# Ten dummy matmuls in four hops, and another spread of two chunk inversions

## The chip, the core and the metric

The kernel runs on one core of one Trainium2 chip. The metric is the device time of one execution in microseconds (us); lower is better. The engines of the core run side by side and wait for each other by semaphores: TensorE (PE: matmuls, with PEld for its weight loads), VectorE (DVE), ScalarE (ACT), GpSimd (POOL) and SyncE (SP), which issues most of the DMAs.

## The reference

A delta-rule attention (4 batches, 8 heads, 768 positions, head size 48) is followed by a feed-forward block with a quick GELU (384 to 2048 to 384) over the 3072 tokens:

```python
k_n = k / (np.linalg.norm(k, axis=-1, keepdims=True) + 1e-06)
state = np.zeros((B, H, D, D))
for t in range(S):
    y[:, :, t] = einsum('bhd,bhde->bhe', q[:, :, t], state)
    v_old = einsum('bhde,bhd->bhe', state, k_n[:, :, t])
    state = state + beta * einsum('bhd,bhe->bhde', k_n[:, :, t], v - v_old)
x = y.transpose(0, 2, 1, 3).reshape(B * S, H * D)
h = x @ w_in
out = (h * (1.0 / (1.0 + np.exp(-1.702 * h)))) @ w_out
```

The two weights arrive as 64-bit floats, and the kernel converts them itself.

## The kernel before, in words

**Units.** The sequence is cut into 6 chunks of 128 positions. A chunk of one batch, with all 8 heads, is a unit; unit n is chunk n // 4 of batch n % 4, so there are 24. Inside a chunk the recurrence is a triangular system. Its four diagonal 32x32 blocks per head are inverted on DVE (`invert`, L460), and the rest is solved by blocks on PE: `solve` multiplies a block of values V with the inverse XB, `below` multiplies the result with the Gram matrix G into psR, and `rest` (L665) subtracts psR from V on DVE, so that the next block can be solved. `together` (L862) puts one such hop of two or three units side by side. From chunk 1 on, `scores` also gives psQ, of which a part is subtracted from V.

**Inversion.** `invert` is a generator that is advanced by hand, with `ahead_of(inverting, n)` for n groups and `run(inverting)` for what is left. From chunk 2 on it works on two units at a time (64 partitions) in 25 groups: one multiplies NT, the Gram blocks, by beta; 15 small ones are each a TENSOR_TENSOR and a TENSOR_REDUCE that grow from 64x2 to 64x450; four make NT from P and four make YB from P (64x256 to 64x1024); the last one makes YS and issues four DMAs on SP: two of YS to DRAM (Yd) and two back into XB, turned.

**Feed-forward.** It is cut into generators too: `hidden` (ph, then GELU to gT), `written` (po, then the output), and `all_written` (L794) for the first chunk. `all_written` runs while w_out is still being converted on DVE (`conversion`): after every two matmuls of po it calls `fill(3)`, three steps of conversion, and, where not all three could be made, one group of the inversion.

**Order.** Up to chunk 2, nearly all instructions are pinned to the order in which the Python code makes them, and each engine works strictly in its order. After the opening the code makes these parts: two hop paths of 8 hops each for the four units of chunk 0 (L1078 to L1084 for the first pair, where `warm` adds dummy matmuls on a bf16 identity, which nobody reads), then a loop of 22 steps (L1139 on) that inverts chunk 1 and feeds PE with ph, with the norms of unit 9 (`ninth`, three steps), and then `woven(n)` for n = 3 to 24, called a slot here. A slot has three hops. The first carries unit n alone with the last blocks of unit n - 1, the second starts unit n + 1, and after the third the outputs of unit n - 1 are formed. Feed-forward work is put between the hops (`spend`). SOON (L904) and STEPS (L903) say how many groups of the inversion follow the first hop, the second hop, and the outputs.

Units 8 and 9 are inverted from slot 4 on. What is left of it after slot 6 is issued at once there:

```python
        if n % HB == 0 and n > B:
            run(inverting)
```

The inversion of units 10 and 11 starts in slot 7, and its last groups are issued at the end of slot 8. Unit 8's inverse is first needed in the second hop of slot 7, that of unit 10 in the second hop of slot 9.

`prepare` (L420) is run within a slot for unit n + 5: it transposes its keys, makes G (half copied from PSUM by ACT, half by DVE), and writes G through DRAM (Nd) into NT; the second of these DMAs waits on SP for the first to land. In slot 6 it is issued ahead of what `run(inverting)` adds. The keys are normalized before that (`normalize_mixed`, from slot 7 on `normalize`): ssq and rn on DVE, a power on POOL, and a product that gives KN.

Of the kernel before, what the change touches and what calls it, by code (L numbers as in the profile page):

```python
# [18 lines left out]
def kernel(  # L19
# [21 lines left out]
    B, H, S, D = q.shape  # L41
# [16 lines left out]
    NW, NY, NU = 14, 26, 11  # L58
# [81 lines left out]
    def warm(n):  # L140
        ps = ps_moe.tile([128, 256], F32, tag="moe", name="ps_warm")
        for _ in range(n):
            pe.matmul(ps, lhsT=ones[:, 0:128], rhs=ones, start=True, stop=True)
# [52 lines left out]
    def fetch_out(f):  # L196

        if f in outside:
            slot = outside[f]
            if slot not in slots and slot[:2] == "gT":  # L200
                slots[slot] = spare("raw").bitcast(I32)[:, 0 : 2 * DM]
            elif slot not in slots:
                slots[slot] = wk.tile([128, 2 * DM], I32, tag=slot[:2].strip("2"), name="raw", bufs=3)
            words = slots[slot]
        else:
            words = raws[:, inside[f] * DM : (inside[f] + 2) * DM]
        places[f] = as_raw(words, (1, DM))
        if order.index(f) >= FC // 2:
            asked[1][f] = asked[0]
        other_queue(  # L210
            out=as_rows(places[f])[:, 0], in_=moe_w_out[f * 128 : (f + 1) * 128, :]
        )
# [95 lines left out]
    def fill(n):  # L308
        all_done = True
        for _ in range(n):  # L310
            asked[0] += 1
            all_done = next(converting, False) and all_done
        return all_done
# [142 lines left out]
    def spare(name):  # L456
        t = wk.tile([128, FQ, NTH], F32, tag="gT", name=name, bufs=GB)
        return t.rearrange("p f t -> p (f t)")
# [334 lines left out]

    def all_written(c, gTs):  # L794

        turns[1] = turns[2] = True
        po = [
            (ps_moe if i < HB else ps_seq[1]).tile([128, DM], F32, tag="moe" if i < HB else "seq", name="po")
            for i in range(B)
        ]  # L800
        for n, f in enumerate(order):
            ahead = order[min(n + 2, FC - 1)]
            while ("out", ahead - ahead % 2 if 4 <= ahead < 8 else ahead) not in done:
                fill(1)
            for i in range(B):
                pe.matmul(
                    po[i], lhsT=gTs[i // HB][f // FQ][:, f % FQ, i % HB * C : (i % HB + 1) * C],
                    rhs=w_out[:, f, :], start=(n == 0), stop=(n == FC - 1),
                )
                if i % HB == HB - 1 and (n < FC - 1 or i < B - 1):  # L810
                    if not fill(3):
                        ahead_of(inverting, 1)
                    yield 1.3
            if f == 3:
                fetch_out(9)
                fetch_out(13)
        turns[2] = False
        rest = spare("o")
        os = [wk.tile([128, DM], F32, tag="o", name="o") for _ in range(HB)]
        os += [rest[:, i * DM : (i + 1) * DM] for i in range(HB)]  # L820
        for i in (2, 3, 0, 1):
            act.copy(os[i], po[i])
        for i in (2, 3, 0, 1):
            beside(out=out[i * S + c * C : i * S + (c + 1) * C, :], in_=os[i])
        yield 1.3
# [15 lines left out]
    def ahead_of(work, n):  # L841
        for _ in range(n):
            next(work, None)
# [18 lines left out]
    def together(solves, belows):  # L862

        solves = [(X, blk) for X, blk in solves if X]
        belows = [(X, blk) for X, blk in belows if X]
        psU = bank("psU") if solves else None
        psR = bank("psR") if belows else None
        for h in range(H):
            for X, blk in solves:
                X.solve(blk, h, psU)  # L870
            for X, blk in belows:
                X.below(blk, h, psR)
        for X, blk in solves:
            X.solved(blk, psU)
        for X, blk in belows:
            X.rest(blk, psR)
# [24 lines left out]
            debt[0] -= done  # L901

    STEPS = (9, 5, 3, 3, 3, 3)  # L903
    SOON = {B - 1: (0, 0, 0), B: (0, 3, 3), B + 1: (1, 1, 1), B + 2: (1, 2, 2)}  # L904
    begun = {}

    def woven(n, share):
# [18 lines left out]
        ahead = STEPS[:3] if n % HB == 1 else STEPS[3:]  # L926
        ahead = SOON.get(n, ahead)

# [95 lines left out]
    def values_scaled(s, hs):  # L1024
        for h in hs:
            act.mul(s.V[:, h, :], s.V[:, h, :], zs[:, 4, s.b, h : h + 1])
# [48 lines left out]
    for i in range(2 * NB):  # L1075
        together(*next(path))
        ahead_of(preparing, 1)
        fill(1 + i % 2 if i else 5)  # L1078
        if 4 <= i < 8:
            values_scaled(pair[HB + (i - 4) // 2], range(i % 2 * NP, i % 2 * NP + NP))  # L1080
        if i in (3, 5):
            pair[HB + (i - 3) // 2].select()
        warm(NU if i < 3 else NU // 2)
        ahead_of(preparing, 1)  # L1084
    for n, s in enumerate(pair[:2]):
        put_out(s, 2 - n)
# [8 lines left out]
    def feed(n=1):  # L1095
        for _ in range(n):
            while ffn and next(ffn[0], None) is None:
                ffn.pop(0)
# [39 lines left out]
    ninth = normalize_mixed(2 * B + 1)  # L1138
    for i in range(22):  # L1139
        ahead_of(inverting, 1)  # L1140
        if i in (14, 17, 20):
            next(ninth)
        if i < 18:
            feed()
        if i in (2, 3, 4, 7, 8, 9, 10):
            fetch_out(i - 2 if i < 5 else i - 3)
# [3 lines left out]
    def beside_conversion(work):  # L1150
        for cost in work:
            fill(4 if ("in", 3, 1) in done else 2)
            yield cost

    queue = [beside_conversion(w) for w in ffn] + [all_written(0, gTs)]
    for n in range(B - 1, len(units) + 1):
        woven(n, 20.8 if n > 6 else 13.0)
# [32 lines left out]
```

## Time and profile before

| | |
|---|---|
| runs | 769.76, 770.48, 774.15 us, median 770.48 |
| the profiled execution | 768.38 us, of which the span of instructions is 766.7 |
| PE busy | 743.1 us, 97% of the span |
| DVE busy | 438.1 us, 57% |
| mean granted TensorE clock | 0.98 |
| ps_warm in the hops (42 to 85 us) | 84 matmuls |

By stage of the kernel, from the answers for single stretches (us busy):

| stretch, us | PE | DVE | clock | what runs |
|---|---|---|---|---|
| 0 to 42 | 34.71 | 33.66 | 0.67 | opening, chunk 0 inverted |
| 42 to 100 | 51.65 | 51.55 | 1.00 | both hop paths |
| 100 to 140 | 39.96 | 37.11 | 1.00 | chunk 1 inverted, ph |
| 140 to 190 | 48.57 | 45.86 | 1.00 | slots 4 to 6, conversion of w_out |
| 190 to 202 | 8.81 | 10.76 | 0.86 | the rest of slot 6's inversion |
| 202 to 245 | 41.56 | 22.59 | 1.00 | slots 7 and 8 |
| 245 to 767 | 517.83 | 236.53 | 1.00 | the other slots, and feed-forward at the end |

A time beside an engine's instruction says how long it was busy; the bracket at the end of a line of the timeline gives the idle time of that engine before it, and what ended it. The TensorE clock is granted by the chip, 1.00 being full speed.

### The profile page before, as it was taken

The page shows a single profiled execution, that of the slowest core. Times are in us where ns is not written, and L with a number is a line of the kernel's source. Part 1 is how long each engine was busy: PE and PEld are TensorE (multiplying, and loading weights), DVE is VectorE, ACT ScalarE, POOL GpSimd, SP SyncE. Part 2 cuts the span into 40 slices and gives each one's busy share as a digit, 9 for nine tenths or more (in the row PEclk, how much of TensorE's full clock was granted, in tenths as well). Part 3 has the DMA queues.
Part 4 walks back from the last instruction along what each step waited for, and adds up shares of the span by engine and source line. Part 5 has one row for each costly group of instructions (what it writes and reads, how often), then busy time and mean ns, then how long its engine had stood idle before and what let it go on. Part 6 is the DMA issues. An engine that isn't in the chain of part 4 may idle for free.

```text
span 766.7 us, 19461 instructions
## 1 busy us (share of the span) xinstructions
PE 743.1 (97%) x8508; PEld 558.2 (73%) x8508; DVE 438.1 (57%) x896; ACT 239.8 (31%) x535; POOL 134.0 (17%) x141
## 2 busy tenths in 40 slices
PE   7888999999899999999999999999999999999998
PEld 6666788666577687687688678678678677687684
DVE  6999898999556566566566566566566521000000
ACT  4557524433233233233133133124123132121110
POOL 6133301312012122122132121230200000000000
PEclk8599999999999999999999999999999999999999
DMA  9965355632332232132142142042030020000000
GB/s 163 174 117 113 82 152 131 165 89 58 65 85 56 56 75 56 42 90 56 36 95 57 35 96 56 23 109 57 22 81 10 23 43 2 17 11 1 27 1 21
DMA packets 131125, 50.78 MB, mean 66 GB/s; under 512 B 106432, under 2 KB 127040, under 8 KB 131040
## 3 DMA queue, kind: packets, MB, share of 16 engines
q1 hardware_dynamic: 127424, 37.34, 23.5%
q0 software_dynamic: 3040, 11.41, 5.6%
q8 instruction: 67, 1.10, 0.6%
q10 hardware_dynamic: 576, 0.79, 0.3%
q14 instruction: 18, 0.15, 0.1%
HBM read 32.08 MB, written 16.25 MB: 63 GB/s over the span
## 4 chain that ended last, share of the span: by engine, by line
PE 77%; DVE 13%; issue 5%; ACT 2%; POOL 2%; DMA 2%; DVEq 0%; POOLq 0%; ACTq 0%; SPq 0%
PE po L102 30%; PE ph L102 26%; PE psY L102 5%; PE psU L102 4%; PE psQ L102 3%; DVE P L102 3%; PE psR L102 2%; PE psG L102 2%; DVE YB L102 2%; PE psT L102 2%; DVE tmp L102 1%; DVE NT L102 1%; DVE w_out L102 1%; DVE w_in L102 1%; POOL rn L102 1%
## 5 line engine op out<-in xcount | busy, mean ns | idle before, releaser
L102 PE MATMUL po<-w_out,gT 128*128 128x384 f32 x768 | 262.5, 493 | 0.0
L102 PE MATMUL ph<-xT,w_in 128*128 128x256 f32 x1152 | 261.4, 383 | 0.3
L102 PEld LDWEIGHTS ph<-xT,w_in 128*128 128x128 f32 x1152 | 214.7, 190 | 32.5 <-issue 1.7
L102 PEld LDWEIGHTS po<-w_out,gT 128*128 128x128 f32 x768 | 142.2, 191 | 92.3 <-issue 3.7
L102 DVE TENSOR_TENSOR V<-V,psR 128x384 f32<-128x384 f32 (+2 forms) x72 | 40.1, 557 | 190.4 <-PE psR L102 189.6
L102 ACT ACTIVATE gT<-ph 128x512 f32<-128x512 f32 x96 | 56.6, 596 | 146.2 <-PE ph L102 146.0
L102 ACT COPY US<-psU 32x384 f32<-32x384 f32 x92 | 43.2, 470 | 145.9 <-PE psR L102 78.3
L102 DVE TENSOR_TENSOR P<-NT,YB 64x8 f32<-64x8 f32 (+26 forms) x178 | 84.3, 474 | 4.7 <-DVE YB L102 0.3
L102 PEld LDWEIGHTS psU<-V,XB 32*32 32x32 f32 x1536 | 58.4, 104 | 36.3 <-issue 26.5
L102 DVE TENSOR_REDUCE YB<-P 64x4 f32<-64x8 f32 (+27 forms) x178 | 77.2, 434 | 6.1
L102 PE MATMUL psU<-V,XB 32*32 32x48 f32 x1536 | 69.7, 203 | 4.4 <-DVE V L102 4.2
L102 PE MATMUL psR<-US,G 32*32 32x48 f32 x2576 | 62.8, 204 | 1.0 <-issue 0.5
L647 POOL TENSOR_SCALAR_AFFINE_SELECT M<-M 128x1024 f32<-128x1024 f32 x20 | 26.5, 1326 | 195.4 <-DVE M L102 161.0
L102 PEld LDWEIGHTS psR<-US,G 32*32 32x32 f32 x2576 | 53.4, 104 | 2.0 <-issue 1.3
L102 PE MATMUL psQ<-QS,kT 48*128 48x176 f32 (+1 forms) x384 | 38.7, 343 | 3.6 <-ACT QS L102 3.6
L102 PEld LDWEIGHTS psQ<-QS,kT 48*128 48x128 f32 x384 | 31.9, 209 | 7.3 <-ACT QS L102 5.4
L102 DVE TENSOR_TENSOR P<-NT 64x256 f32<-64x256 f32 (+7 forms) x44 | 36.3, 824 | 0.4
L102 DVE TENSOR_REDUCE NT<-P 64x64 f32<-64x1024 f32 (+7 forms) x44 | 35.3, 803 | 1.5
L102 PE MATMUL psG<-kT 48*128 48x128 f32 x384 | 32.1, 304 | 1.2 <-ACT G L102 1.2
L87 POOL DMA_DIRECT2D KN<-in_k_dram x13 | 12.4, 950 | 114.8 <-PE psY L102 105.7
L102 ACT COPY o<-po 128x384 f32<-128x384 f32 x24 | 11.4, 479 | 61.5 <-issue 37.3
L102 ACT COPY M<-psQ 128x256 f32<-128x256 f32 x68 | 23.0, 376 | 23.8 <-DVE V L102 17.7
(102 smaller groups left out, 614.8 us busy)
## 6 DMA issues: line engine op xcount, KB each, us to landing
Nd<-G SPq DMA_DIRECT2D x16, 512.0 KB, 3.5
QP<-in_q_dram SPq DMA_DIRECT2D x24, 192.0 KB, 4.0
V<-in_v_dram SPq DMA_DIRECT2D x24, 192.0 KB, 3.3
out_dram<-o SPq DMA_DIRECT2D x20, 192.0 KB, 2.0
raw<-in_moe_w_out_dram POOLq DMA_DIRECT2D x9, 384.0 KB, 3.9
KN<-in_k_dram POOLq DMA_DIRECT2D x14, 192.0 KB, 3.5
w_out<-in_moe_w_out_dram POOLq DMA_DIRECT2D x7, 384.0 KB, 4.8
NT<-Nd SPq DMA_DIRECT2D x20, 128.0 KB, 2.6
```

The source lines that it names most:

```text
L87: dma(out=dst[n % len(dst)][:, :, 0:D], in_=src[b, :, c * C : (c + 1) * C, :].rearrange("h p d -> p h d"),)
L102: return lambda *a, **kw: tc.keep_in_program_order(op(*a, **kw))
L647: (pool if self.n < B else nc.gpsimd).affine_select(out=self.M, in_=self.M, compare_op=ALU.is_gt, fill=0.0, base=0, pattern=[[0, H], [1, 1 ...
```

## The change

1. In hops 3 to 6 of the first pair, `warm` makes 10 dummy matmuls instead of 5, 20 more in all.
2. In `all_written`, a group of the inversion follows only every second time that `fill(3)` could not make all its steps.
3. In slot 5, two groups follow at each of the three places instead of one.
4. In slot 7, the inversion of units 10 and 11 gets 0, 9 and 5 groups at the three places; before it was 9, 5 and 3 by STEPS.
5. The second and third step of `ninth` are called at i = 15 and 19 instead of 17 and 20.

```diff
     def all_written(c, gTs):
 
+        spare_turns = [0]
         turns[1] = turns[2] = True
...
                 if i % HB == HB - 1 and (n < FC - 1 or i < B - 1):
-                    if not fill(3):
+                    spare_turns[0] += not fill(3)
+                    if spare_turns[0] > 1:
+                        spare_turns[0] = 0
                         ahead_of(inverting, 1)
                     yield 1.3
...
-    SOON = {B - 1: (0, 0, 0), B: (0, 3, 3), B + 1: (1, 1, 1), B + 2: (1, 2, 2)}
+    SOON = {B - 1: (0, 0, 0), B: (0, 3, 3), B + 1: (2, 2, 2), B + 2: (1, 2, 2), B + 3: (0, 9, 5)}
...
-        warm(NU if i < 3 else NU // 2)
+        warm(NU if i < 3 else NU - 1 if i < 7 else NU // 2)
...
-        if i in (14, 17, 20):
+        if i in (14, 15, 19):
             next(ninth)
```

In the order of the built programs, TensorE's instructions are the same but for the 20 dummies. On DVE the same instructions stand in another order from the start of the inversion of units 8 and 9 to the end of that of 10 and 11. On SP, the four DMAs of Yd and XB of units 8 and 9 move from between the DMAs of xT to behind the DMA NT<-Nd of slot 6. On ACT one copy to NT moves, that of the inversion of units 10 and 11, from ahead of slot 8's first hop to behind its copies of M.

## Prediction, made before the changed kernel ran

> **What bounds the kernel now.** I read the page first: shares, then slices.
>
> ```profile
> PE 743.1 (97%) x8508; PEld 558.2 (73%) x8508; DVE 438.1 (57%) x896; ACT 239.8 (31%) x535; POOL 134.0 (17%) x141
> ...
> PE   7888999999899999999999999999999999999998
> ...
> DVE  6999898999556566566566566566566521000000
> ```
>
> PE is full from slice 13 (about 245 us) to the end, DVE nearly full from 20 to 200 us. PE's instructions keep their order and number but for the dummies, so the time changes by what PE's idle and slow-clock time changes. I therefore listed PE's idle times after 42 us in the timeline, with what ended each; these are from slots 6 and 7, with the same po x8 of slot 5 ahead of them.
>
> ```profile
> 177.28 2.85 PE L102 MATMUL po<-w_out,gT 128*128 128x384 f32 x8
> ...
> 193.93 0.95 PE L102 MATMUL psT<-ident,KN 128*128 128x128 f32 x4 [2.07 <-DVE KN L102]
> 194.68 4.18 PE L102 MATMUL po<-w_out,gT 128*128 128x384 f32 x8
> ...
> 201.29 0.66 PE L102 MATMUL psY<-QS,ST 48*64 48x128 f32 x14 [0.63 <-DVE V L102]
> ...
> 224.27 0.66 PE L102 MATMUL psT<-ident,KN 128*128 128x128 f32 x4 [1.33 <-POOL KN L331]
> ```
>
> PE stood 2.07 us for the keys of KN. Then eight po took 4.18 us, in slot 5 2.85. The windows say why:
>
> ```profile
> 190.00:194.00 4.00, 1.93 (x41) 0.99 (x30) 3.69 (x10) 0.94 (x2) 0.00 (x0) 1.00 0.26 49
> 194.00:198.00 4.00, 4.00 (x10) 2.55 (x11) 3.93 (x5) 0.60 (x1) 0.00 (x0) 0.57 0.00 0
> ```
>
> The third column from the right is the granted clock: after the pause it fell to 0.57. What DVE did meanwhile is in its timeline.
>
> ```profile
> 190.44 0.41 DVE L102 TENSOR_TENSOR P<-NT,YB 64x256 f32<-64x256 f32 x1
> 190.88 0.41 DVE L102 TENSOR_REDUCE NT<-P 64x64 f32<-64x256 f32 x1
> 191.39 0.42 DVE L102 TENSOR_TENSOR P<-NT 64x256 f32<-64x256 f32 x1
> 191.84 0.41 DVE L102 TENSOR_REDUCE YB<-P 64x64 f32<-64x256 f32 x1
> 192.28 0.56 DVE L102 TENSOR_TENSOR V<-V,psR 64x384 f32<-64x384 f32 x1
> ...
> 193.32 0.56 DVE L102 TENSOR_TENSOR KN<-KN,rn 128x384 f32<-128x384 f32 x1
> ...
> 203.88 0.36 DVE L102 TENSOR_TENSOR ST<-psY,ST 128x192 f32<-128x192 f32 x1 [2.64 <-ACT xT L102]
> ...
> 209.90 0.56 DVE L102 TENSOR_TENSOR V<-V,psR 32x384 f32<-32x384 f32 x1 [4.61 <-PE psR L102]
> ...
> 217.07 1.22 DVE L102 TENSOR_TENSOR NT<-NT,bI 64x1024 f32<-64x1024 f32 x1 [4.94 <-DMA NT<-Nd]
> ```
>
> V and KN queue behind groups of the inversion that nobody needs yet, while DVE stands idle for 2.64 and 4.61 us soon after. And in slot 7 the inversion of units 10 and 11 stands at DVE's head and waits 4.94 us for its DMA, with V and rn behind it; POOL's KN waits for rn, PE for KN (1.33).
>
> **What the Trainium skill says.** "TensorE: Matmul & The Clock Gate", "What's actually happening": the clock has a half-rate and a full state, judged over free-running windows of about 3.4 us of PE activity. The trace agrees in kind: 0.57 in the window above. As its phase is free, other executions may drop elsewhere; no run shown says where. "DMA: Bandwidth & Descriptors", "Two DMAs through the same engine are not ordered": a dependent DMA has to wait for the first one's semaphore; so here SP issues NT<-Nd at 213.87, 4.9 after Nd<-G (208.96). "Perfetto Trace Analysis", "Identifying the Most-Contended Engine", warns that busy PE is not PE at its peak; hence I count only idle and slow time, not shares.
>
> **The change part by part.**
>
> *Dummies.* Eleven ps_warm in a row take 1.38 us and five 0.72, so one costs 0.11 and five more 0.55 a hop. They stand ahead of waits for V of 1.18, 0.62, 0.53 and 1.03 us in hops 3 to 6: hidden but for some 0.02. Without that cover it would be 20 x 0.11 = 2.2 us. The clock is 1.00 throughout 42 to 100 us in this execution, so nothing is gained in its sum. In others a drop there may be avoided; I bound that from 0 to 1.7 us, the price of the drop above.
>
> *Steps of `ninth`.* No engine's order changes by it: the inversion has ended by i = 14. Zero.
>
> *Slots 4 and 5.* I laid the new DVE order over the old times, each instruction not before its producer. NT<-NT,bI (1.21) moves from 147.09 to behind KN (153.5), and DVE loses that time, since it waits for a DMA of w_out at 151.57 anyway. The small groups that go out balance it, but a w_out step that ACT answers comes 0.4 later, and ACT's QS behind it; psQ at 160.10 slips by 0.4, its second half for V by 0.1 more. Loss: 0.5. The later V of slots 4 and 5 come at 158.2, 170.0 and 174.3, each when PE needs it or before.
>
> *Slot 6.* Seven groups and YS were done or queued ahead of the last V. Now V 64x384 comes right after psR (190.9 with the loss above), rn and KN end at 192.5, and PE wants KN at 192.4. The 2.07 gap shrinks to 0.15, and its drop of the clock goes: psT 0.95 - 0.66 = 0.3 and po 4.18 - 2.85 = 1.3. The wait for V ahead of psY (0.63) goes too. Gain: 1.9 + 1.6 + 0.6 = 4.1. The groups of 64x256 and 64x512 (2.2) fit into the idle 2.64 ahead of ST. 64x768, 64x1024 and YS (1.9 + 2.4 + 1.2 = 5.5) follow G, in a hole of 4.6: V 32x384 of slot 7 comes 0.9 late. Behind it waits the second half of psQ; usually V ends about 0.2 ahead of it, so PE loses 0.7.
>
> *SP.* Yd and XB of unit 8 now go behind NT<-Nd. Counted from the end of psG (204.52 before): xT's six issues, then Nd<-G at +3.1; it lands in 3.5 to 4.8, NT is issued at +7.4, Yd at +7.8, lands in 2 to 4, XB is issued at +10.4 to 12 and lands in 2.7 to 4: +13.2 to 16. Slot 8 has the same sequence and comes to about +13. Unit 8's solve follows psG by 219.27 - 204.52 = 14.75, with the 0.7 above 15.4. I take no wait; the bounds are -0.6 late to +2.2 early. What waits behind it would be PE itself.
>
> *Slot 7.* rn stands ahead of NT<-NT,bI now, KN comes 2.0 us before psT: the 1.33 gap goes. NT's DMA, its G earlier, lands before DVE gets there. Eight groups end some 1 us before the next V is due.
>
> *Slot 8.* Now five groups, 0.8 + 1.4 + 1.9 + 2.4 + 1.2 = 7.8, follow G where before there were two (3.7); the hole to V of slot 9 is about 7.1, so by the same reckoning psQ loses 0.45. Later slots are unchanged.
>
> Sum: gains 4.1 + 1.3, losses 0.5 + 0.7 + 0.45: 3.8 us off 768.38, which is 764.6. The median of the runs lies 2.1 above that execution; for the changed kernel I allow half of it, since the dummies and the missing pause leave the clock less to drop at: 765.6.
>
> **The rivals.**
>
> *XB late (no change).* The DMAs behind NT take the long end, unit 8 waits 2 us, the clock drops once (1.7): 765.6 + 3.7 = 769.3. For it: only 1.5 us of margin, and output DMAs land at the same time. Against: slot 8 does the same in time.
>
> *Dummies in the way (no change).* The V of the hops come earlier than in this execution, the dummies show for 2.2: 767.8. Against: all four gaps end with DVE V, and DVE hardly idles there.
>
> *Slower.* SP holds Yd until NT can be issued; if Nd<-G waits for G or its traffic, XB slips one for one. It decides once it lands 1.5 us after the reckoned time; the gain is eaten after about 2 more with a drop of the clock, and at 7.5 late, 765.6 + 7.5 + 1.7 = 774.8, the kernel is slower than can be mistaken. For it: the queue is blocking; against: the longest landing of any of these DMAs here is 4.9.
>
> **How the numbers follow.** The forecast has 0.60, XB late 0.17, the dummies 0.12, slower 0.11. About 0.5% (3.9 us) can be told from no change, so faster means below 766.6. The forecast's own range is 763 to 767.5, nine tenths of it below the bound; with a few hundredths from the rivals, faster 0.56, same 0.33, slower 0.11. The range runs from 762.8 (a drop in the hops avoided, no psQ waits) to 769.8, which takes in both milder rivals.
>
> **What would show it.** Right: no PE idle over 0.3 us before psT of slot 6, clock 1.00 from 186 to 204 us, no wait for KN in slot 7, PE's wait before psQ of slots 7 and 9 under 1 us, hops of the first pair as long as before. Wrong: PE waiting for XB in slot 7, a new drop of the clock, a longer first pair, or PE idling between 140 and 180 us by more than 1 us over before.

## The result, and the profile after

| | before | after |
|---|---|---|
| runs | 769.76 to 774.15 us, median 771.09 (4) | 762.70 to 763.34 us, median 763.11 (4) |
| ratio | | 0.989, 95% interval 0.986 to 0.9921 |
| the profiled execution | 768.38 us | 763.34 us |
| PE busy, DVE busy | 743.1, 438.1 us | 744.1, 438.6 us |

The kernel became 1.1% faster. Forecast were 765.6 us, 0.9937 of the median then known. The two profiled executions differ by 5.0 us, the medians by 8.0. These are two quantities, and they are taken one by one below.

The timeline of TensorE after the change, slots 6 and 7 (start, duration, instruction, idle time before and what ended it):

```profile
191.58 0.66 PE L102 MATMUL psT<-ident,KN 128*128 128x128 f32 x4 [0.28 <-DVE KN L102]
192.07 2.75 PE L102 MATMUL po<-w_out,gT 128*128 128x384 f32 x8
...
206.48 0.86 PE L102 MATMUL psQ<-QS,kT 48*128 48x176 f32 x6 [0.48 <-DVE V L102]
...
219.23 0.66 PE L102 MATMUL psT<-ident,KN 128*128 128x128 f32 x4 [0.33 <-POOL KN L331]
```

The pause of 2.07 us is 0.28, the eight po take 2.75 instead of 4.18, the wait of 1.33 for KN in slot 7 is 0.33, and one wait is new: 0.48 ahead of the second half of psQ. The windows of the same stretch show no drop of the clock. (A line of a window gives its length, then the busy us of PE, PEld, DVE, ACT and POOL, each with its instructions, then the clock, the DMA share and GB/s.)

```profile
190.00:194.00 4.00, 3.72 (x14) 2.06 (x14) 3.83 (x8) 1.41 (x3) 0.00 (x0) 1.00 0.25 49
194.00:198.00 4.00, 3.51 (x121) 2.65 (x119) 3.59 (x8) 0.47 (x1) 0.00 (x0) 1.00 0.02 4
```

DVE's timeline after the change:

```profile
189.93 0.56 DVE L102 TENSOR_TENSOR V<-V,psR 64x384 f32<-64x384 f32 x1 [0.46 <-PE psR L102]
...
204.61 1.22 DVE L102 TENSOR_TENSOR YS<-YB,bI 64x1024 f32<-64x1024 f32 x1
205.86 0.56 DVE L102 TENSOR_TENSOR V<-V,psR 32x384 f32<-32x384 f32 x1
...
216.24 0.56 DVE L102 TENSOR_TENSOR V<-V,psR 64x384 f32<-64x384 f32 x1 [8.14 <-PE psR L102]
```

V of slot 6 now waits for PE (0.46) and not PE for it. The rest of the inversion fills the hole up to YS, and V of slot 7 follows YS without a break: that is where the new 0.48 comes from. In slot 7 DVE waits 8.14 us for PE, where it waited 4.94 for NT's DMA before.

SyncE's queue shows the transfers that were moved behind NT<-Nd:

```profile
207.41 0.33 SPq L102 DMA_DIRECT2D NT<-Nd  x1
207.82 1.31 SPq L102 DMA_DIRECT2D Yd<-YS  x2
211.62 1.00 SPq L102 DMA_DIRECT2D XB<-Yd  x2
```

The first XB lands 2.6 us after its issue, at 214.2; its solve starts at 215.24 without a wait. The margin is 1.0 us.

To place the 5.0 us I compared the start of every DVE subtraction of V in both profiles; "V stands at -0.56" means that it starts 0.56 us earlier than in the profile of before. The changed kernel stands at +0.2 us in the first hop path, at -0.65 us at 135 us, -0.56 in the first hop of slot 6, -4.92 in its third, -5.4 in the first hop of slot 8, -5.11 from its third on and to the end. (In between a single V may lie off by up to 1 us.) The lines behind the largest step, the third hop of slot 6, are these, first before and then after the change:

```profile
199.43 1.22 DVE L102 TENSOR_TENSOR YS<-YB,bI 64x1024 f32<-64x1024 f32 x1
200.68 0.56 DVE L102 TENSOR_TENSOR V<-V,psR 128x384 f32<-128x384 f32 x1
```

```profile
195.76 0.56 DVE L102 TENSOR_TENSOR V<-V,psR 128x384 f32<-128x384 f32 x1 [0.31 <-PE psR L102]
```

Before, V followed the last group of the inversion without a break; now DVE waits for PE.

### The profile page after: what moved, and what is told of

Its sections match the earlier page's. It is cut to its first block, busy times and chain, and to the rows that moved or that the text cites. A ratio compares the mean times of both kernels' runs of the same rounds, so it can differ in the third digit from the quotient of the medians.

```text
span 761.6 us, 19501 instructions
## 1 busy us (share of the span) xinstructions
PE 744.1 (98%) x8528; PEld 559.7 (73%) x8528; DVE 438.6 (58%) x896; ACT 239.9 (31%) x535; POOL 134.4 (18%) x141
## 4 chain that ended last, share of the span: by engine, by line
PE 82%; DVE 8%; issue 5%; ACT 2%; POOL 2%; DMA 1%; POOLq 0%; DVEq 0%; ACTq 0%
PE po L102 29%; PE ph L102 27%; PE psY L102 5%; PE psU L102 5%; PE psQ L102 5%; PE psG L102 3%; PE psT L102 3%; PE psR L102 3%; PE ps_warm L102 2%; DVE w_out L102 2%; DVE tmp L102 1%; DVE V L102 1%; DVE w_in L102 1%; DVE YB L102 1%; DVE P L102 1%
## 5 line engine op out<-in xcount | busy, mean ns | idle before, releaser
L647 POOL TENSOR_SCALAR_AFFINE_SELECT M<-M 128x1024 f32<-128x1024 f32 x20 | 24.4, 1220 | 192.8 <-DVE M L102 160.2
L102 PEld LDWEIGHTS psG<-kT 48*128 48x128 f32 x384 | 28.0, 210 | 3.6 <-ACT G L102 2.1
```

What stands on the lines that cost most here:

```text
L102: return lambda *a, **kw: tc.keep_in_program_order(op(*a, **kw))
L647: (pool if self.n < B else nc.gpsimd).affine_select(out=self.M, in_=self.M, compare_op=ALU.is_gt, fill=0.0, base=0, pattern=[[0, H], [1, 1 ...
```

## The experiments

All were measured against the kernel before in the same series. Each series (e1 to e4, e5 to e8, e9 to e12) ran on a chip of its own; the medians of before differ by up to 1.1 us between them. "Low clock" counts executions whose mean granted clock is 0.971 or less.

| label | what | median us (runs) | span of the runs | low clock | ratio, 95% interval |
|---|---|---|---|---|---|
| e1 | dummies alone | 770.08 (22) | 767.2 to 772.5 | 0 | 0.998, 0.9965 to 0.9996 |
| e2 | all but the dummies | 765.51 (10) | 764.6 to 770.5 | 1 | 0.9932, 0.9907 to 0.9958 |
| e3 | slot 7 alone | 769.23 (22) | 767.2 to 773.0 | 3 | 0.9978, 0.9961 to 0.9996 |
| e4 | slots 4 to 6 alone | 765.24 (8) | 764.2 to 772.0 | 3 | 0.9933, 0.9901 to 0.9965 |
| e5 | the changed kernel | 764.69 (6) | 763.5 to 766.2 | 0 | 0.9926, 0.9909 to 0.9942 |
| e6 | changed, no dummies in hops 3 to 7 | 764.50 (6) | 763.9 to 765.5 | 3 | 0.9923, 0.9908 to 0.9937 |
| e7 | all_written alone | 766.95 (9) | 765.9 to 769.0 | 4 | 0.9959, 0.9945 to 0.9972 |
| e8 | changed, 17 dummies in slots 5, 6 | 763.16 (5) | 762.9 to 763.8 | 0 | 0.9906, 0.9891 to 0.992 |
| e9 | before, the pause filled | 771.42 (14) | 769.4 to 774.3 | 4 | 0.9997, 0.9978 to 1.0016 |
| e10 | the changed kernel | 763.39 (6) | 762.9 to 765.1 | 0 | 0.9894, 0.9866 to 0.9921 |
| e11 | as e8 | 763.40 (6) | 762.7 to 763.9 | 0 | 0.9888, 0.9861 to 0.9915 |
| e12 | as e8, 1, 2, 3 groups in slot 6 | 762.46 (6) | 762.2 to 763.0 | 0 | 0.9879, 0.9852 to 0.9906 |

The kernel before had medians of 770.72 (49 runs), 770.23 (14) and 771.35 (19) in the series of e1 to e4, e5 to e8 and e9 to e12. Of these 82 runs 34 have a low clock, with a median of 773.8; the 8 with 0.979 or more have 768.3. So its profiled execution (768.38, clock 0.98) was one of its best.

**e1: the dummies alone**

```diff
-        warm(NU if i < 3 else NU // 2)
+        warm(NU if i < 3 else NU - 1 if i < 7 else NU // 2)
```

> The kernel before with the 20 dummies alone. Two theories of the 3 us that the runs gained over what the two profiled executions show (768.38 to 763.34, so 5.0, while the medians went from 771.1 to 763.1, so 8.0). Theory A: the dummies hold TensorE's clock in executions in which it falls in the first pair; then this gains about 3.0 (ratio 0.996) and the clock of every execution is 1.00 between 42 and 100 us. Theory B: the pause in slot 6 costs some executions more than the profiled one; then the dummies alone give nothing (ratio 1.000), and the runs scatter over several us as those of before.

Median 0.6 us less, and none of 22 runs has a low clock where 20 of the 49 beside them have: theory A in kind, but with a gain of 0.3 to 2.7 by the interval, less than its 3.0. The scatter of several us stays, as theory B has it. The profiled execution is one of the longest (771.95): its clock falls at 174 to 178 us and at 201 to 208, and V loses 2.7 and 2.6 us there (more under e9). The hops themselves are no shorter: every V from 47 to 76 us stands at about +0.17. A step of 0.75 comes at 77 to 80 us, in the second pair, far from any edit. The timeline of before shows what is missing there afterwards:

```profile
78.18 0.20 PE L102 MATMUL psR<-US,G 32*32 32x48 f32 x1
78.21 0.20 PE L102 MATMUL psU<-V,XB 32*32 32x48 f32 x1
78.96 0.23 PE L102 MATMUL psR<-US,G 32*32 32x48 f32 x2 [0.54 <-issue]
```

In the middle of a hop TensorE stops for 0.54 us with nothing that the profile shows to wait for. From the second V of the second pair to the third it is 2.75 to 3.32 us in the six profiles with the old dummies, of which before's is the longest, 2.46 to 2.59 in the seven with the new, and 2.57 without any in hops 3 to 7 (e6). But most of the step comes without the new dummies too: e3, e7 and e9, with the old ones, show 0.54 to 0.58 us of it against before, and the view lists no such stop in them. It lists one in before, e2 (0.48) and e4 (0.25). So the dummies can be given the 0.2 to 0.3 us that every profile with the old ones is longer; that they also keep the stop away (none in seven, against three in six) is likely and not shown. What TensorE stops for was not settled.

**e2: all but the dummies**

The whole change without e1's line.

> All of the change but the dummies. Theory A: 5.0 us less than before by the profile's gain, ratio 0.9935, with a scatter of several us left. Theory B: all 8.0 us, ratio 0.9896, and runs within 1 us of each other.

5.2 us less by the medians: theory A's number, and the scatter is there. The profiled execution happened to be the longest of the ten (770.47). Its windows show why:

```profile
174.00:178.00 4.00, 2.40 (x29) 1.77 (x26) 3.90 (x10) 0.59 (x2) 0.00 (x0) 0.71 0.02 4
178.00:182.00 4.00, 4.00 (x45) 3.68 (x41) 2.07 (x6) 1.33 (x5) 0.91 (x1) 0.50 0.04 6
182.00:186.00 4.00, 4.00 (x7) 2.18 (x8) 3.09 (x6) 0.59 (x1) 0.00 (x0) 0.51 0.61 174
```

The clock falls in slot 5 and stays at half for some 10 us. The V ahead of it stands at +1.97 against before's profile and the first of slot 6 at +6.61: 4.6 us for one drop. TensorE's timeline has two waits close together there, 0.61 for ACT and 0.99 for V before psY. So the clock can fall in slot 5 too, and in some executions only: the profiles of e1, e3, e5 and e7 have a shorter drop between 162 and 178 us, the other nine have none in slot 5.

**e3: slot 7 alone**

```diff
-    SOON = {..., B + 2: (1, 2, 2)}
+    SOON = {..., B + 2: (1, 2, 2), B + 3: (0, 9, 5)}
```

> The kernel before with the entry for slot 7 alone (0, 9, 5 groups). Both theories: PE's wait of 1.33 us for the keys KN in slot 7 goes or falls to 0.3, the pause of 2.07 in slot 6 with its slow clock stays: 1.0 to 1.3 us less (ratio 0.9985), which is near what can be told apart.

The wait for KN is 0.33, and V moves from +2.16 in slot 6 to +1.08 in slot 8: 1.1 us, as reckoned. The medians give 1.5, within the interval.

**e4: slots 4 to 6 alone**

```diff
-                    if not fill(3):
+                    spare_turns[0] += not fill(3)
+                    if spare_turns[0] > 1:
+                        spare_turns[0] = 0
...
-    SOON = {B - 1: (0, 0, 0), B: (0, 3, 3), B + 1: (1, 1, 1), B + 2: (1, 2, 2)}
+    SOON = {B - 1: (0, 0, 0), B: (0, 3, 3), B + 1: (2, 2, 2), B + 2: (1, 2, 2)}
```

> The kernel before with the edits to slots 4 to 6 alone (every second group in all_written, 2, 2, 2 in slot 5). Pause and slow clock in slot 6 go. By the prediction's sum the wait for KN in slot 7 stays, and this gains 2.7 in the profile; theory A then 2.7 to 3.7 in the medians, theory B 6.7. A third reading: NT of units 10 and 11 lands some 6 us earlier here, so that it holds up nothing in slot 7 even ahead of V and rn; then this alone gives what the spread gives, and the entry for slot 7 adds nothing to it.

The median is e2's within 0.3, so the third reading holds for the time as far as these runs can tell. It holds only half for its reason. NT still made DVE wait 4.49 us:

```profile
213.29 1.22 DVE L102 TENSOR_TENSOR NT<-NT,bI 64x1024 f32<-64x1024 f32 x1 [4.49 <-DMA NT<-Nd]
...
218.40 0.56 DVE L102 TENSOR_TENSOR V<-V,psR 64x384 f32<-64x384 f32 x1
```

V and KN follow late behind it, yet PE's wait for KN is 0.34 as in e2. In the profile the entry for slot 7 is worth 0.6 us on top of this part (V from slot 6 to the end: 0.4 lost here, 0.2 gained in the changed kernel), of 1.1 alone.

**e5 and e10: the changed kernel again**

> The changed kernel once more, on one chip with the others of this row. If the four runs that it has (762.7 to 763.3) are what it always gives, the median stays at 763.1 and the scatter under 1 us. If they happened to meet no drop of the clock, the median is 764 to 765 and some runs lie at 766 to 770, as with the parts; then the ratio is nearer 0.992 than 0.989.

> The changed kernel a third time, beside the next two on one chip: by its ten runs so far 763.6, with some runs at 766 in which the clock fell in slots 5 or 6.

764.69 and 763.39. With its first four runs it has 16, median 763.5; ten of them lie below 764, the longest is 766.22. The four of the result were on the good side, but the second ratio is again 0.989: there the kernel before is 1.1 us longer than beside e5, with 10 of 19 low clocks in place of 4 of 14, and the changed kernel is 1.3 shorter. The profile of e5 has a drop in slot 5, at 174 to 178 us, and V goes from -0.41 to +1.13 there; that of e10 has none.

**e6: no dummies at all in hops 3 to 7**

```diff
-        warm(NU if i < 3 else NU - 1 if i < 7 else NU // 2)
+        if i < 3:
+            warm(NU)
```

> The changed kernel with no dummy matmuls at all in hops 3 to 7 of the first pair (45 fewer). If the dummies hold TensorE's clock there: drops to 0.5 within 50 to 70 us in the profile, more runs with a mean clock of 0.97 or less, 2 to 5 us more than the changed kernel. If the hops are only waits for DVE and the clock doesn't depend on them: the same time as the changed kernel within 0.5 us, with the hops as long as before.

Both readings are half right. The clock falls, from 54 to 70 us, the longest drop of any profile here:

```profile
54.00:62.00 8.00, 6.56 (x94) 5.70 (x95) 7.64 (x14) 6.82 (x18) 4.55 (x4) 0.58 0.82 183
62.00:70.00 8.00, 8.00 (x93) 7.24 (x91) 7.12 (x13) 6.02 (x17) 2.28 (x1) 0.56 0.38 67
```

And it costs little. V stands at -0.36 against before at 47 us, and at the same -0.36 at 61: up to there DVE, busy for 7.64 of the 8 us, sets the pace, and a TensorE at half speed keeps up. Behind that TensorE is busy all the time, and the next V, the first of the second pair, waits for it (in the changed kernel it doesn't) and stands at +0.53:

```profile
74.31 0.55 DVE L102 TENSOR_TENSOR V<-V,psR 128x384 f32<-128x384 f32 x1 [0.97 <-PE psR L102]
```

Part of this comes back. From 47 to 85 us e6 loses 0.55 to 0.66 us to the profiles with the new dummies (the changed kernel, e1, e5, e8, e10 to e12), which have no stop at 79 us either. Against the profile of before, which has the stop, nothing shows: -0.52 at 85 us. The median, 764.50, is that of e5 beside it; 0.6 us is less than these runs can tell.

So a low mean clock alone is hardly a loss. In kernels with the old dummies it goes with longer times all the same (e7: 767.8 to 769.0 for its four, 765.9 to 767.0 for the others). The profile of e7 has a drop at 62 to 67 us that costs nothing (V at +0.48 ahead of it, at +0.25 behind) and one at 162 to 165, around which V goes from +0.60 to +1.88. No execution with a low clock and the old dummies was profiled, so where those runs lose their time stays open.

**e7: all_written alone**

The first four lines of e4's diff (and the line that sets spare_turns to 0).

> The kernel before with the edit of all_written alone (a group of the inversion every second time). V and KN of slot 6 no longer stand behind the inversion, so the pause of 2.07 us and its slow clock go. But some 8.5 us of groups now follow G, where the hole in DVE is 4.6: V of slot 7 comes about 3.9 late and psQ waits 3.5 for it. By my reckoning of holes this gains 4.1 and loses 3.5: 770 against 770.7. If instead the wait of psQ is hidden, it gains like the edits to slots 4 to 6 together: 765.2.

766.95, and neither number. The reckoning of DVE's hole is right: V of slot 7 moves from -1.83 to +2.04, 3.9 late. But PE waits only 0.98 ahead of psQ, and for something else:

```profile
210.07 0.86 PE L102 MATMUL psQ<-QS,kT 48*128 48x176 f32 x6 [0.98 <-ACT US L102]
```

So a late V doesn't hold psQ one for one, though the expectation had it so. Slot 6 gains 3.7 (V from +1.88 to -1.83). The first V of slot 7 is late, the ones behind it are not: from slot 7's second V to the end they stand at -1.49, so that slot 7 as a whole costs 0.3.

**e8 and e11: 17 dummies in slots 5 and 6**

`warm` takes the PSUM tile as a second argument here and in e9.

```diff
         turns[1] = turns[2]
+        if n == B + 1:
+            warm(9, ps_big.tile([128, 256], F32, tag="big", name="ps_warm"))
         run(D_.scored)
...
         if A:
+            if n in (B + 1, B + 2):
+                warm(4, ps_big.tile([128, 256], F32, tag="big", name="ps_warm"))
             A.queries()
```

> The changed kernel with 17 dummies more in slots 5 and 6: 9 ahead of psQ of slot 5, where PE waits 1.05 us, and 4 each ahead of psY, where it waits 0.5 to 0.8. If the scatter of the runs comes from the clock falling after these thin stretches (as the profiles of two parts show at 162 to 178 us), the runs lie closer together and no profile has a clock of 0.5 between 150 and 190 us; the dummies themselves cost 0 to 0.5. If the clock falls by chance or for another reason, the scatter stays that of the changed kernel.

> The changed kernel with the 17 dummies in slots 5 and 6, again. If these dummies keep the clock up: all runs within 1 us at 763.2, none above 764.5, while the changed kernel beside it has runs above 764.5. If its five runs were luck: the same scatter as beside it.

Eleven runs in two series lie between 762.73 and 763.89, none with a drop in slots 5 or 6 in its profile; of the changed kernel's 16 runs six lie above. The median hardly moves (763.4 against 763.5 over all runs; 763.16 against 764.69 and 763.40 against 763.39 beside each other). In these runs the dummies take away the long ones and cost nothing that can be measured.

**e9: the pause filled**

```diff
         spend(share / 6)
+        if n == B + 2:
+            warm(17, ps_big.tile([128, 256], F32, tag="big", name="ps_warm"))
         next(P, None)
```

> The kernel before with 17 dummies ahead of psT of slot 6, so that TensorE is busy in the pause of 2.07 us while DVE's order, and so the pause itself, stay. If the slow clock behind the pause is made by the pause, the clock stays 1.00 from 190 to 204 us, the eight po after it take 2.85 us and not 4.18, and the kernel gains the 1.6 us of the prediction: 768.6 to 769 where before has 770.2 to 770.7, with V of the later hop now the next thing to wait for, since DVE's burst ends when it did: then part of the 1.6 comes back as a wait for V ahead of psY (0.6 before, up to 2.2 now), and the gain is between 0 and 1.6. If the clock falls in any case, nothing is gained.

The kernel before, with TensorE busy in the pause; its timeline:

```profile
191.34 2.02 PE L102 MATMUL ps_warm<-ident 128*128 128x256 bf16 x17
193.57 0.66 PE L102 MATMUL psT<-ident,KN 128*128 128x128 f32 x4 [0.21 <-DVE KN L102]
194.06 2.75 PE L102 MATMUL po<-w_out,gT 128*128 128x384 f32 x8
...
200.94 1.12 PE L102 MATMUL psY<-QS,ST 48*64 48x128 f32 x14 [2.33 <-DVE V L102]
```

The clock stays up and the eight po take 2.75. Nothing is gained: PE reaches psY earlier, waits 2.33 us for V instead of 0.63, and the clock falls there instead, from about 200 to 206 us.

That the pause makes the slow clock isn't shown by this. In the profile of e1 the pause is open, 2.07 us as in before, and yet the clock stays up behind it and falls only at the longer wait for V:

```profile
195.28 0.66 PE L102 MATMUL psT<-ident,KN 128*128 128x128 f32 x4 [2.07 <-DVE KN L102]
195.77 2.75 PE L102 MATMUL po<-w_out,gT 128*128 128x384 f32 x8
...
202.65 1.13 PE L102 MATMUL psY<-QS,ST 48*64 48x128 f32 x14 [2.32 <-DVE V L102]
```

```profile
196.00:200.00 4.00, 3.51 (x89) 2.07 (x88) 3.93 (x5) 1.04 (x2) 0.00 (x0) 1.00 0.01 4
200.00:204.00 4.00, 1.68 (x20) 1.10 (x22) 2.53 (x3) 0.00 (x0) 0.00 (x0) 0.69 0.29 65
204.00:208.00 4.00, 4.00 (x46) 3.91 (x44) 0.36 (x1) 0.81 (x3) 0.94 (x1) 0.50 0.01 1
```

In e3 the clock falls after the open pause as in before (eight po in 4.34 us). So behind an open pause it fell in two of three profiles.

V itself doesn't depend on all this: it stands at -0.35 all through slot 6 in e9 and at +1.36 all through slot 6 in e1. TensorE's waits for KN and V, 2.07 and 2.32 in e1, are together the same 4.4 us as 2.07, the 1.6 of the slow clock and 0.63 in before. The 4.4 us that the changed kernel gains in slot 6 are DVE's lateness, and PE's slow clock was inside them. Where the clock falls at the wait for V, it costs more on top: against before, V of slot 7 stands 2.5 (e9) and 2.6 us (e1) later than V of slot 6 did. So slot 6 can cost an execution more than the profiled one, as theory B of e1 has it.

**e12: one group more ahead of ST**

```diff
-    SOON = {..., B + 2: (1, 2, 2), B + 3: (0, 9, 5)}
+    SOON = {..., B + 2: (1, 2, 3), B + 3: (0, 9, 5)}
```

> The same, with three groups instead of two at the last place of slot 6, so that 64x768 stands ahead of ST and G and only 64x1024 and YS follow G. DVE has 0.56 us of idle time ahead of ST; V of slot 7 comes that much earlier, and PE's wait of 0.48 ahead of psQ in slot 7 goes. If that wait is on the path: 0.5 less than with 17 dummies alone, 762.7. If G, 1.3 us later, holds up Nd and with it XB: no gain or some tenths lost.

This is e11 with one group more at the last place of slot 6. It takes 0.94 us less than e11 beside it, where 0.5 was expected; the runs of the two overlap only from 762.7 to 763.0. It takes 0.9 less than the changed kernel. DVE's and TensorE's timelines:

```profile
203.52 1.22 DVE L102 TENSOR_TENSOR YS<-YB,bI 64x1024 f32<-64x1024 f32 x1
204.98 0.56 DVE L102 TENSOR_TENSOR V<-V,psR 32x384 f32<-32x384 f32 x1 [0.24 <-PE psR L102]
```

```profile
204.84 1.62 PE L102 MATMUL psQ<-QS,kT 48*128 48x176 f32 x16
```

V of slot 7 waits for PE again, and psQ runs through in 1.62 us. In the changed kernel its two parts took 1.16 and 0.86 with 0.48 between them, from 204.84 to 207.34: the late V cost 0.88 us, and not only the wait. V stands at -4.92 here and at -4.04 there. This kernel is faster than both before and the changed one.

## Why the prediction was right or wrong

**Slot 6: right in place and size.** Foreseen were 4.1 us, V moved by 4.36 (-0.56 to -4.92). The parts were named by TensorE's waits: 1.9 pause, 1.6 clock, 0.6 V. e9 and e1 show that they can't be had one by one; it is one quantity, how late DVE is with V. Where all of DVE's lateness goes, the sum over PE's waits gives the same number. That the sum came out right doesn't show that each part was a gain of its own.

**Slot 7: right in its parts.** KN's wait fell by 1.0 (1.3 foreseen); V of slot 7 is 0.88 late (0.9) and costs psQ 0.88 (0.7), of which 0.48 is a wait. XB came in time with 1.0 us to spare (1.5): the rival "XB late" didn't come. On SP, Nd<-G was issued 4.3 us after the end of psG, not 3.1, and XB at 12.0, the late end of its range.

**Slots 4, 5, 8 and 9: too pessimistic for this execution.** For slots 4 and 5 0.5 us of loss were laid down; V moves from -0.65 to -0.56, 0.1. That is in part luck: with the same slots 4 and 5 it loses 0.1 to 0.65 in e4, e6, e8, e10, e11 and e12, which have no drop there, and 1.8 in e2 ahead of its drop. For slot 9 0.45 were laid down; V there is 0.55 late, and 0.55 earlier again at the next, so PE lost nothing. Within slot 8, where no loss was foreseen, 0.3 are lost.

**The dummies: hidden, as said, in all four hops.** Of the profile's 5.0, 0.65 arises at 77 to 80 us, for which the prediction has no term. A good part of it is luck: before's profiled execution was the longest there of the six with the old dummies, and three of the others were 0.54 to 0.58 shorter. The dummies' own part is 0.2 to 0.3, as far as the profiles show it.

So the sum came to 5.0 in place of 3.8: 0.65 from outside the argument, 0.4 from the loss in slots 4 and 5 that was charged and not taken, 0.3 from slot 6. Slots 7 to 9 together gave 0.2, as charged; their errors cancel.

**The step that failed is the allowance for the clock:** "The median of the runs lies 2.1 above that execution; for the changed kernel I allow half of it". The median of the four runs lay 0.2 below the changed kernel's own profiled execution, so the distance was not halved but gone; over 16 runs the median is 0.2 above. Of the 2.5 us between the forecast and the measured median, 1.3 are in this term and 1.2 in the sum above. The mechanism was named, a clock with less to drop at, and its size was taken too small. It was half the distance of one execution from a median of three, and that execution was among the best tenth of 82, while the runs of before reach up to 778. With 5.0 in the sum and no distance left the forecast would have been 763.4. The shortest runs of both kernels differ by 5.3 (767.96 and 762.70), about as the profiles do; the medians of all their runs differ by 7.2 (770.7 and 763.5). So what the term missed lies in what makes the longer runs of before longer.

One source of it is shown. The prediction counted what slot 6 costs in one execution, with the drop behind the pause. In e1 and e9 the clock falls at the wait for V instead, and 2.6 and 2.5 us more are lost. The changed kernel has no such wait, and none of its three profiles (the result, e5, e10) has a drop in slots 6 or 7. How many executions of before take that course was not measured, so how much of the term it explains stays open. The drops also have no one price: the prediction takes 1.6 us in slot 6 and 1.7 elsewhere, and the profiles show from nothing (e7 at 62 us) to 4.6 (e2). (Its five groups in slot 8 add up to 7.7 and not 7.8, which changes nothing.)

That the dummies take away the executions with a low clock is shown by count: these are 34 of 82 in before, 4 of 14 in e9 and 11 of 49 in e2, e3, e4 and e7, and none in 55 of the kernels with the new dummies (e1, e5, e8, e10, e11, e12 and the result). What that is worth is shown only for e1, 0.6 us of the median; what a low-clock execution loses where isn't shown.

## What to carry to other kernels

Put work that has no due date behind the instruction that another engine waits for, in the hole that the same engine has a few microseconds later; price it by how late that one result comes, and not by the sum of the other engine's waits and its slow clock. Before a forecast is set on one profiled execution, ask where in the scatter of the runs it lies: where the clock falls in some executions and not in others, an edit can take away losses that the one profile doesn't contain. An effect seen by comparing two profiles should be looked for in a third: the step at 77 to 80 us looked like the dummies' own until profiles without them showed most of it, and the slow clock looked like the pause's own until a profile with the pause had none. Dummy matmuls in TensorE's short waits took away long runs here (e8, e11); where TensorE waits for a late result of another engine they gained nothing (e9).

## What the runs showed of the hardware

- The clock can fall at waits shorter than the 3.4 us window of the Trainium skill ("TensorE: Matmul & The Clock Gate", "What's actually happening"): after 2.07 us in before, at 2.32 us in e1 and 2.33 in e9, at 0.61 and 0.99 us close together in e2. It need not: after the same 2.07 us it stayed at 1.00 in e1. The drop lasted about 3.5 us in before and 10 in e2. That it comes in some executions and not in others fits the page's free-running window; the runs show no window. None of the fourteen profiles has a drop between 210 and 750 us; in before's TensorE is busy for 99% of the time from 245 us on.
- Sixteen us with the clock at 0.57 cost about 0.6 us in e6, where DVE was 92% busy, and nothing up to 61 us, as long as DVE set the pace. Ten us at half cost 4.6 in e2.
- TensorE stopped for 0.54 us between two matmuls of one hop, with no wait on record, in before (0.48 in e2, 0.25 in e4). The view lists it in none of the seven profiles with 20 dummies more, nor with 25 fewer (e6), but in e3, e7 and e9, which have the dummies of before, neither.
